# Diagonals of five chunks by quadrant products, one selection per chunk, and a new order for the start of a linear attention kernel with a feed-forward layer

## The chip, the cores and the metric

The kernel runs on one core of a Trainium2 chip. The metric is the device time of one execution in microseconds; the median of three runs stands for a kernel. Five engines work from queues of their own, each in the order written: TensorE (PE; its weight loads are listed as PEld), VectorE (DVE), ScalarE (ACT), GpSimd (POOL) and SyncE (SP, which here only issues DMA transfers). They wait for each other through semaphores.

## The reference

```
for t in range(768):                      # batch 4, 8 heads, head size 48
    cur = (u * k_t) outer v_t
    y_t = r_t @ (state + cur)
    state = w_t[:, None] * state + k_t outer v_t
x = y as (4*768 tokens) x (8*48 = 384)
h = max(x @ w1, x @ w2, x @ w3)           # 384 -> 768
out = h @ w_out                           # 768 -> 384
```

All is float32. The decay w lies between 0.8 and 0.95, so products of it over a chunk become small.

## The kernel before, in words

**Chunks.** The 768 tokens of a batch are cut into 6 chunks of 128, so there are 24 chunks, numbered k = 0 to 23. The eight heads lie as four pairs: one head of a pair on partitions 0 to 47, the other on 64 to 111. Four chunks make a block of 512 tokens, and there are six blocks. Per chunk these steps are done, each named by one letter (line of the code behind it):

- b (365): a DVE scan backwards over the decay, g. Its first column per pair, the decay of the whole chunk, is copied by ACT to `dec`.
- s (373) and f (379): the reciprocal of that decay, held above a floor of 1e-13, starts a forward scan f on DVE.
- r (385): three DVE products scale k by g (two instructions) and r by f (one), in place in the loaded table `tin`.
- X (447): PE makes the scores ("gram"), k' against r', in 64x64 quadrants, into two PSUM banks.
- d, D, e (401, 413, 423): the diagonal term, the sum of r*u*k over the head. For the first six chunks (`CS`) d is a DVE product r*k in two instructions, D sums it over the partitions by small PE matmuls against u, and e copies the eight sums per token to `cs` by ACT. For later chunks POOL makes two products and DVE a sum. e then spreads `cs` on the diagonal of the weight tile `a`: by eight ACT instructions for chunks 0 and 1, by two POOL selections (`affine_select`) for all others. e also issues the next chunk's load of v (and, where needed, of r and k as they are).
- M (465): DVE's `copy_predicated` puts the scores above the diagonal into `a`, one instruction for each of the two banks.
- T (475): PE transposes k'; ACT copies the result (kn) out of the bank "tu".
- R, U, S (488, 496, 510): result from the state, update of the state into the same bank "tu", and its scaling by the decay (four ACT instructions for chunks 0 to 3).
- V, Z (531, 551): PE applies `a` to v, in two halves.
- E (554): ACT copies the result y to x. In the third and fourth chunk of a block it also issues transfers x<-x inside the on-chip memory, three on SP and, in the first block, three on ACT.
- c (397): a check; ACT squares g and f in place and sums them. The sums are judged near the end.

**Feed-forward.** A block has 18 groups (six slices of 128 hidden columns by three weight matrices), each three products of 128x128 by 128x512, and then 24 products for `w_out`. The first block is multiplied in plain float32, later ones in split float32r. Group results lie in three PSUM banks, `psm`, used in turn (the fillers and D use them too). The first of three groups is copied out by ACT, the other two are taken up by DVE with a maximum. The first two groups of the first block begin on chunks 0 to 2 alone (384 columns, line 148) and are completed with the last 128 columns (line 156) when chunk 3 has arrived.

**Weights.** The 24 weight tiles arrive as pairs of 32-bit words. Each is put together by one ACT instruction (`split_w1`, line 311) and two DVE instructions (`split_w2`, 320 and 322).

**Order.** All order is written out by hand. `FRONT` (line 70) is the first stretch: a letter with a digit is a step and its chunk, `W3` three filler matmuls on a zero tile (line 588), `n` a load of r, k, w, `w` a weight load on SP, `i` one `split_w1`, `c` without a digit one whole weight, `p` one of the two early groups, `m` one group, `x` the hand-over of the first block. Then `START`, and `TURN` and `ORD` for each later chunk (line 594), interleaved with groups. An order is an order per engine: what stands behind a waiting instruction of its engine waits too. Ten filler matmuls come ahead of `FRONT`.

Of the kernel before, what the change touches and what calls it, by code (L numbers as in the profile page):

```python
# [69 lines left out]
FRONT = ("b0 s0 f0 d0 W2 D0 W3 r0 X0 e0 T0 W3 c0 b1 s1 d1 D1 U0 f1 W2 R0 e1 S0 M0 V0 Z0 E0 n3 r1 "  # L70
# [25 lines left out]
def kernel(ctx: ExitStack, tc, tin, nat, u_flat, u_pair, v_t, w_all, out, ytr):  # L96
# [107 lines left out]
    with ExitStack() as fast:  # L204
# [711 lines left out]
```

## Time and profile before

| what | value |
| --- | --- |
| median of three runs | 412.45 us (410.98 to 412.71) |
| span of the profiled execution | 409.3 us |
| own time of the profiled execution | not given; its span lies 3.15 us under the median |
| instructions | 9188 |
| TensorE busy | 399.6 us (98%) |
| VectorE busy | 276.2 us (67%) |
| ScalarE busy | 158.2 us (39%) |
| GpSimd busy | 76.7 us (19%) |

Busy time is a sum over the whole span; a busy TensorE may also be running fillers. What a stage waits for is read from the timelines and from the chain of waits, which is followed back from the last instruction.

### The profile page before, as it was taken

To read this page: it belongs to the slowest core of one execution; us is meant where nothing else is said; L and a number is where in the kernel's file an instruction comes from. 1 tells how busy PE (TensorE), PEld (TensorE's weight loads), DVE (VectorE), ACT (ScalarE), POOL (GpSimd) and SP (SyncE) were. 2 spreads that over 40 slices of the span, in tenths; PEclk is the share of its full clock that TensorE was granted. 3 is DMA by queue.
4 is the path that set the end of the run, shared out by engine and by line. 5 is a ranking of instruction groups with operands and counts; after the bars stand their busy time and mean duration, and the time that the engine had idled before them with its cause. 6 is when DMAs were issued, how large, how long until landed. Compare 5 with 4: busy or idle time off the path is not lost.

```text
span 409.3 us, 9188 instructions
## 1 busy us (share of the span) xinstructions
PE 399.6 (98%) x3726; PEld 314.7 (77%) x3726; DVE 276.2 (67%) x504; ACT 158.2 (39%) x356; POOL 76.7 (19%) x92
## 2 busy tenths in 40 slices
PE   6999999999999999999999999999999999999995
PEld 2766554556688889988889988889988888978894
DVE  7988799989869969776778557688565622233320
ACT  2955343333435542434533644533532321322211
POOL 2111041244123113123123113223113200000000
PEclk9999999999999999999999999999999999999999
DMA  8868993630542140694562686841550000300002
GB/s 199 228 183 231 342 345 142 226 105 21 183 148 70 59 126 3 195 295 138 156 194 88 180 257 218 229 145 40 164 185 2 2 2 2 97 2 0 2 3 78
DMA packets 24270, 54.09 MB, mean 132 GB/s; under 512 B 3328, under 2 KB 9920, under 8 KB 24224
## 3 DMA queue, kind: packets, MB, share of 16 engines
q1 hardware_dynamic: 20160, 43.34, 35.0%
q10 hardware_dynamic: 4064, 10.13, 8.2%
q8 instruction: 30, 0.49, 0.5%
q14 instruction: 16, 0.13, 0.1%
HBM read 47.55 MB, written 4.72 MB: 128 GB/s over the span
## 4 chain that ended last, share of the span: by engine, by line
PE 93%; ACT 2%; DMA 1%; SPq 1%; issue 1%; ACTq 1%; POOL 1%; DVE 0%; POOLq 0%
PE psm L168 56%; PE psm L188 17%; PE gram L460 5%; PE y L542 4%; PE tu L503 3%; PE y L493 3%; PE psm L591 2%; PE tu L480 2%; DMA x<-x 1%; PE psm L419 1%; SPq L569 1%; ACTq L569 1%; PE psm L156 0%; ACT x L560 0%; ACT cv L311 0%
## 5 line engine op out<-in xcount | busy, mean ns | idle before, releaser
L168 PE MATMUL psm<-x_hi,w 128*128 128x512 f32 x540 | 172.9, 394 | 0.2 <-ACT m L199 0.2
L168 PEld LDWEIGHTS psm<-x_hi,w 128*128 128x128 f32 x540 | 101.4, 188 | 22.0 <-ACT m L199 0.8
L168 PE MATMUL psm<-x_lo,w 128*128 128x512 f32 x270 | 105.3, 390 | 0.0
L134 DVE TENSOR_TENSOR m<-psm,m 128x512 f32<-128x512 f32 x60 | 41.2, 686 | 61.0 <-PE psm L168 44.4
L188 PE MATMUL psm<-w,h_hi 128*128 128x384 f32 x288 | 78.2, 364 | 0.0
L438 POOL TENSOR_SCALAR_AFFINE_SELECT a<-cs 64x512 f32<-64x512 f32 x44 | 32.2, 733 | 147.1 <-DVE cs L429 93.0
L168 PEld LDWEIGHTS psm<-x_lo,w 128*128 128x128 f32 x270 | 50.7, 188 | 9.8
L188 PEld LDWEIGHTS psm<-w,h_hi 128*128 128x128 f32 x288 | 51.8, 188 | 6.5 <-DVE w L322 0.4
L168 PE MATMUL psm<-x,w 128*128 128x512 f32 x96 | 42.8, 598 | 0.0
L410 POOL TENSOR_TENSOR kr<-kr 128x384 f32<-128x384 f32 x18 | 22.7, 1262 | 97.8 <-PE y L542 87.4
L560 ACT COPY x<-y 112x512 f32<-112x512 f32 x24 | 14.1, 587 | 68.2 <-PE y L542 67.8
L188 PE MATMUL psm<-w,h_lo 128*128 128x384 f32 x120 | 40.3, 336 | 0.0
L399 ACT ACTIVATE gf<-gf 112x1034 f32<-112x1034 f32 x24 | 25.7, 1070 | 35.0 <-DVE tin L394 34.6
L111 ACT CAST h_hi<-m 128x512 fp32r<-128x512 f32 x30 | 18.6, 622 | 52.9 <-DVE m L134 52.5
L382 DVE TENSOR_TENSOR_SCAN gf<-tin,d_fwd 112x517 f32<-112x517 f32 x24 | 34.9, 1454 | 0.7
L168 PEld LDWEIGHTS psm<-x,w 128*128 128x128 f32 x96 | 17.7, 190 | 20.7 <-issue 19.5
L368 DVE TENSOR_TENSOR_SCAN gf<-tin,d_bwd 112x517 f32<-112x517 f32 x24 | 29.9, 1246 | 3.7 <-DMA tin<-in_tin_dram 3.7
L112 DVE TENSOR_TENSOR h_lo<-m,h_hi 128x512 fp32r<-128x512 f32 x30 | 20.6, 688 | 16.8 <-ACT h_hi L111 16.8
L469 DVE COPY_PREDICATED a<-mask,gram 128x384 f32<-128x384 int32 x48 | 25.3, 580 | 1.2 <-PE gram L460 1.2
L542 PE MATMUL y<-a,v 64*64 64x64 f32 (+3 forms) x768 | 25.4, 246 | 0.6
L542 PEld LDWEIGHTS y<-a,v 64*64 64x64 f32 (+1 forms) x768 | 21.4, 126 | 4.6 <-issue 3.1
L131 ACT COPY m<-psm 128x512 f32<-128x512 f32 x30 | 17.5, 582 | 16.7 <-PE psm L168 9.7
(77 smaller groups left out, 428.2 us busy)
## 6 DMA issues: line engine op xcount, KB each, us to landing
tin<-in_tin_dram SPq DMA_DIRECT2D x23, 448.0 KB, 5.6
w<-in_w_all_dram SPq DMA_DIRECT2D x24, 384.0 KB, 6.9
cv<-in_w_all_dram ACTq DMA_DIRECT2D x24, 384.0 KB, 3.8
kr<-in_nat_dram SPq DMA_DIRECT2D x18, 384.0 KB, 5.8
tin<-in_tin_dram SPq DMA_DIRECT2D x23, 231.0 KB, 3.4
v<-in_nat_dram SPq DMA_DIRECT2D x24, 192.0 KB, 5.3
out_dram<-m SPq DMA_DIRECT2D x23, 192.0 KB, 3.0
x<-x SPq DMA_DIRECT2D x30, 32.0 KB, 2.0
```

Source lines behind the costliest of these rows:

```text
L112: rest = lambda: nc.vector.tensor_tensor(out=lo, in0=src, in1=hi.bitcast(F32), op=ALU.subtract)
L134: nc.vector.tensor_tensor(out=m[:, :], in0=ps[:, :], in1=m[:, :], op=ALU.max)
L168: nc.tensor.matmul(ps[:, :], lhsT=wt[f * 3 + wi][:, ct * 128:(ct + 1) * 128], rhs=xt[:, ct, :], start=(n == 0), stop=(n == KT * len(terms) ...
L188: nc.tensor.matmul(pss[tt][:, 0:DM], lhsT=ht[f][:, tok], rhs=wt[FT * 3 + f][:, :], start=(f == 0 and i == 0), stop=(f == FT - 1 and i == l ...
L368: nc.vector.tensor_tensor_scan(out=gf[0:112, 0, ::-1], data0=t[0:112, 0:WC][:, ::-1], data1=d_bwd[0:112, ::-1], initial=0.0, op0=ALU.mult, ...
L382: nc.vector.tensor_tensor_scan(out=gf[0:112, 1, :], data0=tbuf[k % NB][0:112, 0:WC], data1=d_fwd[0:112, :], initial=0.0, op0=ALU.mult, op1 ...
L399: nc.scalar.activation(out=flat, in_=flat, func=AF.Square, accum_out=acc[0:112, k:k + 1])
L410: nc.gpsimd.tensor_tensor(out=n[:, 0, :], in0=n[:, 0, :], in1=n[:, 1, :], op=ALU.mult)
L438: nc.gpsimd.affine_select(out=a[rows, :, 0:2, :], pattern=[[0, 4], [0, 2], [1, HC]], in_=cs[rows, :].rearrange("p (a b) -> p a b", b=2).un ...
L460: nc.tensor.matmul(to, lhsT=p["kp"][q:q + 48, pr, lo:lo + HC], rhs=p["rp"][q:q + 48, pr, HC * late:C], start=(hh, lo) not in begun, stop=T ...
L469: nc.vector.copy_predicated(out=p["a"][:, 2 * hh:2 * hh + 2, :, :].rearrange("p a b c -> p a (b c)"), mask=mask_b(2), data=p["gs"][hh].rea ...
L542: mm = nc.tensor.matmul(p["y"][64 * half:64 * half + m, hh, j, HC * late:C], lhsT=natt[k][0][lo:lo + HC, h * D:h * D + m], rhs=a[:, j, :] ...
```

## The change

- The diagonal of chunks 0 to 4 (`CS` is 5 now): ACT scales r by u (four instructions of 128 columns, one per pair). PE multiplies raw k against it in the same 64x64 quadrants as the scores, of which only the diagonal is wanted. The result needs two PSUM banks: two of `psm`, or for chunk 4 one of `psm` and the bank "tu". ACT copies each to `a` (256 columns), and two POOL selections keep the diagonal, now for chunks 0 and 1 too. Chunk 5's diagonal goes the way of the later chunks: a load, two POOL products, a DVE sum.
- `a` has its blocks in another order. The block that needs no mask is copied by a step of its own, N (ACT, 512 columns in all; for chunk 3 O, on DVE), and M is one `copy_predicated` of 512 columns.
- The floor of the reciprocal is gone; the sums of the checks are compared by their shifted bits.
- The chunk decay is copied by ACT only for chunks behind the fifth; before, it is read from g itself. The scalings of chunk 0 go to tiles of their own.
- The checks of chunks 0 to 4 come behind the loop of the first four chunks (g has five buffers for it). The loads of v are steps of their own, `l`.
- `FRONT` is written anew: 5 fillers in place of 18, weight loads 2 and 3 between the transfers x<-x of chunks 2 and 3, U of chunk 3 behind the two early groups and D of chunk 4.

```diff
-FRONT = ("b0 s0 f0 d0 W2 D0 W3 r0 X0 e0 T0 W3 c0 b1 s1 d1 D1 U0 f1 W2 R0 e1 S0 M0 V0 Z0 E0 n3 r1 "
-         "W1 X1 d2 D2 e2 w w T1 c1 b2 s2 R1 U1 S1 M1 V1 Z1 E1 f2 r2 "
-         "W4 X2 d3 D3 e3 w n4 w T2 c2 b3 s3 R2 U2 S2 i i M2 V2 Z2 E2 w w f3 r3 "
-         "W3 X3 T3 i R3 M3 x V3 Z3 E3 w w n5 w U3 p p d4 w c n6 w m D4 b4 s4 c c3 S3 m w f4 c e4 m r4 c X4 T4 R4 c4 w w")
-TURN = "b1 d1 w | f1 w | D1 r1 c1 | e1 M0 w | "
-ORD = "w R0 V0 U0 X1 Z0 E0 b2 d2 | f2 n3 w | D2 S0 r2 c2 | e2 M1 w | T1 w | |"
+FRONT = ("b0 s0 f0 d0 W2 D0 r0 e0 d1 b1 X0 N0 T0 l2 n3 W1 s1 D1 f1 R0 e1 d2 M0 V0 U0 S0 Z0 E0 r1 "
+         "b2 X1 N1 T1 w w l3 s2 D2 R1 e2 d3 M1 V1 U1 S1 n4 Z1 E1 f2 r2 "
+         "b3 X2 N2 T2 s3 D3 R2 e3 M2 V2 i U2 S2 Z2 E2 l4 w w f3 r3 "
+         "W2 X3 T3 c R3 O3 x V3 Z3 E3 i w w n5 w p p d4 w D4 e4 c U3 n6 w l5 b4 c0 m s4 c S3 c1 m w f4 c c2 m r4 c X4 N4 T4 R4 c3 c4 w w")
+TURN = "b1 d1 w | D1 f1 w | r1 c1 | e1 M0 w | "
+ORD = "w R0 V0 U0 X1 Z0 E0 N1 b2 d2 | f2 n3 w | D2 S0 r2 c2 | e2 M1 w | T1 w | |"
...
-            nc.scalar.copy(out=dec[k % 2][0:112, :], in_=gf[0:112, 0, 1:WC:WS])
-            prep[k]["gf"] = gf
+            if k > CPH:
+                nc.scalar.copy(out=dec[k % 2][0:112, :], in_=gf[0:112, 0, 1:WC:WS])
+            prep[k].update(gf=gf, dec=dec[k % 2][0:112, :] if k > CPH else gf[0:112, 0, 1:WC:WS])
 
         def prep_start(k):
             gf = prep[k]["gf"]
             sep = d_fwd[0:112, 0:NP * WS:WS]
-            nc.vector.tensor_scalar(out=sep, in0=gf[0:112, 0, 1:WC:WS], scalar1=FLOOR, scalar2=None, op0=ALU.max)
-            nc.vector.reciprocal(sep, sep)
+            nc.vector.reciprocal(sep, gf[0:112, 0, 1:WC:WS])
...
+        def weight_of(k):
+            if "a" not in prep[k]:
+                prep[k]["a"] = a_p.tile([128, 3, 4, HC], F32, name="a")
+            return prep[k]["a"]
+
         def prep_diag1(k):
             if k < CS:
                 t = tbuf[k % NB]
-                prep[k]["kr"] = n = nat_p.tile([128, 2, DM], F32, name="kr")[:, :, :].rearrange("p a b -> p (a b)")[:, 0:NP * C]
-                n, r, q = (z.rearrange("p (a b) -> p a b", a=NP) for z in (n, t[:, WC:WC + NP * C], t[:, WC + NP * C:TC_]))
-                for j in range(2):
-                    nc.vector.tensor_tensor(out=pairs(n, j), in0=placed(r, j), in1=pairs(q, j), op=ALU.mult)
+                n = nat_p.tile([128, 2, DM], F32, name="kr")[:, :, :].rearrange("p a b -> p (a b)")[:, 0:NP * C]
+                prep[k]["ur"] = n = n.rearrange("p (a b) -> p a b", a=NP)
+                for pr in range(NP):
+                    nc.scalar.activation(out=n[0:112, pr, :], in_=t[0:112, WC + pr * C:WC + (pr + 1) * C], func=AF.Identity,
+                                         scale=t[0:112, TC_ + pr:TC_ + pr + 1])
                 return
             n = natt[k][1]
...
         def prep_diag_sum(k):
             if k < CS:
-                n, t = prep[k]["kr"], tbuf[k % NB]
-                prep[k]["ps"] = ps = ps_m.tile([128, HT], F32, name="psm")
-                for pr in range(NP):
-                    for lo in (0, HC):
-                        nc.tensor.matmul(ps[lo:lo + HC, pr:2 * NP:NP], lhsT=n[0:112, pr * C + lo:pr * C + lo + HC],
-                                         rhs=t[0:112, TC_ + 2 * pr:TC_ + 2 * pr + 2], start=(pr == 0), stop=True,
-                                         skip_group_check=True)
+                p = prep[k]
+                raw = tbuf[k % NB][:, WC + NP * C:TC_].rearrange("p (a b) -> p a b", a=NP)
+                p["ps"] = ps = [t[:, 0:4 * HC].rearrange("p (a b c) -> p a b c", a=2, b=2) for t in (
+                    ps_m.tile([128, HT], F32, name="psm"),
+                    ps_tu.tile([128, 512], F32, name="tu") if k == CPH else ps_m.tile([128, HT], F32, name="psm"))]
+                begun = set()
+                for half in range(2):
+                    for late in range(2):
+                        for j in range(2):
+                            for hh in range(2):
+                                pr, q = 2 * half + j, 64 * hh
+                                lo, tok = HC * (late if j else 1 - late), slice(HC * late, HC * late + HC)
+                                nc.tensor.matmul(ps[hh][lo:lo + HC, j, half, :], lhsT=raw[q:q + 48, pr, lo:lo + HC],
+                                                 rhs=p["ur"][q:q + 48, pr, tok], start=(hh, lo) not in begun,
+                                                 stop=True, skip_group_check=True)
+                                begun.add((hh, lo))
 
         def prep_diag2(k):
             ahead("D", k)
-            cs = small.tile([128, LINE], F32, name="cs")[:, 0:H]
+            a = weight_of(k)
             if k < CS:
-                nc.scalar.copy(out=cs[:, :], in_=prep[k]["ps"][:, 0:H])
+                for hh in range(2):
+                    nc.scalar.copy(out=a[:, 0:2, 2 * hh:2 * hh + 2, :].rearrange("p a b c -> p a (b c)"),
+                                   in_=prep[k]["ps"][hh].rearrange("p a b c -> p a (b c)"))
             else:
-                nc.vector.tensor_reduce(out=cs[:, :].rearrange("p (a b) -> p b a", a=2),
-                                        in_=natt[k][1][:, 0, :].rearrange("p (b a d) -> p b a d", a=2, d=D),
+                cs = small.tile([128, LINE], F32, name="cs")[:, 0:H]
+                nc.vector.tensor_reduce(out=cs[:, :].rearrange("p (j h q) -> p q j h", j=2, h=2),
+                                        in_=natt[k][1][:, 0, :].rearrange("p (q j h d) -> p q j h d", j=2, h=2, d=D),
                                         axis=AX.X, op=ALU.add)
-            a = a_p.tile([128, 4, 3, HC], F32, name="a")
-            for q in range(4) if k < EARLY else ():
-                for b in range(2):
-                    nc.scalar.activation(out=a[:, q, b, :], in_=ident2, func=AF.Identity, scale=cs[:, 2 * q + b:2 * q + b + 1])
-            for lo in (0, HC) if k >= EARLY else ():
+            for lo in (0, HC):
                 rows = slice(lo, lo + HC)
-                nc.gpsimd.affine_select(out=a[rows, :, 0:2, :], pattern=[[0, 4], [0, 2], [1, HC]],
-                                        in_=cs[rows, :].rearrange("p (a b) -> p a b", b=2).unsqueeze(3).broadcast_to([HC, 4, 2, HC]),
+                src = a[rows, 0:2, :, :] if k < CS else cs[rows, :].rearrange("p (a b) -> p a b", a=2).unsqueeze(3).broadcast_to([HC, 2, 4, HC])
+                nc.gpsimd.affine_select(out=a[rows, 0:2, :, :], pattern=[[0, 2], [0, 4], [1, HC]], in_=src,
                                         compare_op=ALU.is_equal, fill=0.0, base=0, channel_multiplier=-1)
-            prep[k]["a"] = a
-            if k + 1 < NK:
-                load_nat(k + 1)
+            if CPH < k + 1 < NK:
+                ahead("l", k + 1)
...
+        def views(k):
+            to, gs = weight_of(k), prep[k]["gs"]
+            return to[:, :, :, :].rearrange("p b (h a) c -> p h b (a c)", h=2), gs.rearrange("p h b a c -> p h b (a c)")
+
+        def take_full(k):
+            to, data = views(k)
+            nc.scalar.copy(out=to[:, :, 2, :], in_=data[:, :, 2, :])
+
+        def take_alone(k):
+            to, data = views(k)
+            nc.vector.tensor_copy(out=to[:, :, 2, :], in_=data[:, :, 2, :])
+            take(k)
+
         def take(k):
-
-            p = prep[k]
-            for hh in range(2):
-                nc.vector.copy_predicated(out=p["a"][:, 2 * hh:2 * hh + 2, :, :].rearrange("p a b c -> p a (b c)"), mask=mask_b(2),
-                                          data=p["gs"][hh].rearrange("p a b c -> p a (b c)"))
+            to, data = views(k)
+            nc.vector.copy_predicated(out=to[:, :, 0:2, :], mask=mask_b, data=data[:, :, 0:2, :])
```

## Rows read from the trace of the kernel before

**Rows 1.** The page's engine table: busy time, share of the span, instructions.
```profile
PE 399.6 (98%) x3726; PEld 314.7 (77%) x3726; DVE 276.2 (67%) x504; ACT 158.2 (39%) x356; POOL 76.7 (19%) x92
```

**Rows 2.** Windows: length, busy time of PE, PEld, DVE, ACT, POOL, clock, DMA.
```profile
30.00:40.00 10.00, 9.40 (x63) 6.16 (x64) 8.92 (x18) 6.24 (x16) 1.32 (x2) 1.00 0.79 219
40.00:50.00 10.00, 10.00 (x71) 4.91 (x70) 7.59 (x14) 2.67 (x6) 0.00 (x0) 1.00 1.02 326
```

**Rows 3.** The chain of waits, 31 to 37 us: start, length, what.
```profile
30.94 0.48 ACT x L560
31.44 4.08 DMA x<-x
35.65 1.08 PE psm L156 x6
```

**Rows 4.** Timeline of PE: start, length, line, operation, count, idle before it.
```profile
3.22 5.30 PE L591 MATMUL psm<-warm 128*128 128x512 bf16 x12 [3.22 <-POOL warm L586]
...
9.96 0.90 PE L460 MATMUL gram<-tin 48*64 48x128 f32 x32
...
15.05 0.90 PE L460 MATMUL gram<-tin 48*64 48x128 f32 x32
...
19.94 1.04 PE L591 MATMUL psm<-warm 128*128 128x512 bf16 x4
...
26.54 0.90 PE L460 MATMUL gram<-tin 48*64 48x128 f32 x32
...
31.42 4.04 PE L148 MATMUL psm<-x,w 128*128 128x384 f32 x12
...
37.99 2.74 PE L168 MATMUL psm<-x,w 128*128 128x512 f32 x6
40.66 0.90 PE L460 MATMUL gram<-tin 48*64 48x128 f32 x32
...
50.54 0.63 PE L419 MATMUL psm<-tin,kr 112*64 112x2 f32 x16
```

**Rows 5.** Timeline of DVE, chunks 1 to 3 (L376 is the floor).
```profile
16.46 0.17 DVE L376 TENSOR_SCALAR d_fwd<-gf 112x4 f32<-112x4 f32 x1
...
16.76 1.04 DVE L469 COPY_PREDICATED a<-mask,gram 128x384 f32<-128x384 int32 x2
17.69 1.58 DVE L382 TENSOR_TENSOR_SCAN gf<-tin,d_fwd 112x517 f32<-112x517 f32 x1
...
20.44 0.75 DVE L407 TENSOR_TENSOR kr<-tin 112x256 f32<-112x256 f32 x2
```

**Rows 6.** Timeline of POOL and DVE, at 17 and at 132 us.
```profile
16.80 1.39 POOL L438 TENSOR_SCALAR_AFFINE_SELECT a<-cs 64x512 f32<-64x512 f32 x2 [13.63 <-ACT cs L427]
...
131.62 1.01 POOL L411 TENSOR_TENSOR kr<-kr,u_bc 128x384 f32<-128x384 f32 x1
131.82 1.90 DVE L382 TENSOR_TENSOR_SCAN gf<-tin,d_fwd 112x517 f32<-112x517 f32 x1
```

**Rows 7.** Timeline of ACT, 9 to 38 us.
```profile
9.52 2.02 ACT L435 ACTIVATE a<-ident,cs 128x64 f32<-128x64 f32 x8
...
26.60 0.60 ACT L560 COPY x<-y 112x512 f32<-112x512 f32 x1
...
29.83 0.53 ACT L482 COPY kn<-tu 128x448 f32<-128x448 f32 x1 [2.62 <-issue]
...
33.61 0.66 ACT L311 ACTIVATE cv<-w,minus_two 128x384 f32<-128x384 uint32 x1 [2.20 <-issue]
...
34.79 1.07 ACT L399 ACTIVATE gf<-gf 112x1034 f32<-112x1034 f32 x1
...
35.84 0.86 ACT L519 ACTIVATE sstar<-tu,dec 112x48 f32<-112x48 f32 x4
36.76 0.58 ACT L131 COPY h_hi<-psm 128x512 f32<-128x512 f32 x1
```

**Rows 8.** Line 295's weight loads on SP, 14 to 40 us: issue to landing.
```profile
DMA to landing us min/median/max: 3.1/4.6/9.4
```

More of the change, by code (lines that the diff above doesn't have):

```diff
@@ L84 @@
 CHECK = 2
-FLOOR = 1e-13
-LIMIT = 5e25
+LIMIT_BITS = int(np.float32(5e25).view(np.uint32))
 TENTHS = 7.4999 * 2.0 ** -54
@@ L208 @@
         v_p = pool("v", 3)
-        g_p = pool("g", 2)
+        g_p = pool("g", 5)
         a_p = pool("a", 2)
@@ L217 @@
         cv_p = pool("cv", 3)
-        ps_g = pool("ps_g", 2, space=PSUM)
+        ps_g = pool("ps_g", 1, space=PSUM)
         ps_y = pool("ps_y", 1, space=PSUM)
@@ L356 @@
         nc.vector.memset(mid_top[:, :], -7.0)
+        nc.scalar.copy(out=dec[0][:, 0:1], in_=mid_top[:, :])
         load(1)
@@ L449, in scores @@
             p = prep[k]
-            p["gs"] = gs = [ps_g.tile([128, HT], F32, name="gram") for _ in range(2)]
-            p["gs"] = gs = [g[:, 0:6 * HC].rearrange("p (a b c) -> p a b c", a=2, b=3) for g in gs]
+            both = ps_g.tile([128, 2, HT], F32, name="gram")[:, :, 0:6 * HC]
+            p["gs"] = gs = both.rearrange("p h (a b c) -> p h a b c", a=3, b=2)
             begun = set()
@@ L458, in scores @@
                             lo = HC * (late if j else 1 - late)
-                            to = gs[hh][lo:lo + HC, half, j, :] if late else gs[hh][lo:lo + HC, half, j::2 - j, :]
+                            to = gs[lo:lo + HC, hh, j, half, :] if late else gs[lo:lo + HC, hh, j::2 - j, half, :]
                             nc.tensor.matmul(to, lhsT=p["kp"][q:q + 48, pr, lo:lo + HC],
@@ L540, in values @@
                         h, lo = 4 * half + 2 * j + hh, 64 * row
-                        a = p["a"][lo:lo + HC, 2 * hh + half]
+                        a = p["a"][lo:lo + HC, :, 2 * hh + half, :]
                         mm = nc.tensor.matmul(p["y"][64 * half:64 * half + m, hh, j, HC * late:C],
@@ L569, in result @@
                     eng.dma_start(out=x[lo + 48:lo + 64, j, cols], in_=x[lo + 16 * j:lo + 16 * j + 16, KT, cols])
-        steps = dict(X=scores, M=take, T=transposes, R=from_state, U=to_state, S=state, V=values, Z=values2, E=result, n=load,
+        steps = dict(X=scores, M=take, N=take_full, O=take_alone, l=load_nat, T=transposes, R=from_state, U=to_state, S=state, V=values, Z=values2, E=result, n=load,
                      b=prep_scan_b, s=prep_start, f=prep_scan_f, r=prep_rk, c=prep_check, d=prep_diag1,
@@ L580, in ahead @@
                 steps[step](k)
-        ident2 = cst.tile([128, LINE], F32, name="ident2")[:, 0:HC]
-        for lo in (0, HC):
-            nc.vector.tensor_copy(out=ident2[lo:lo + HC, :], in_=ident[lo:lo + HC, lo:lo + HC])
         warm = cst.tile([128, 128], BF16, name="warm")
@@ L875, in _layout @@
         rows[..., WC + NP * C:TC_] = ks.reshape(B, NCH, D, NP * C)
-        rows[..., TC_ + half:TC_ + 2 * NP:2] = u.reshape(NP, 2, D)[:, half].T
+        rows[..., TC_:TC_ + NP] = u.reshape(NP, 2, D)[:, half].T
     def natural(a):
```

33 lines of the change are left out of this document (20 added, 13 removed).

## The prediction

> **What bounds the kernel now.** The page's engine table comes first: TensorE (PE) is busy 98% of the span, VectorE (DVE) 67%, ScalarE (ACT) 39% [rows 1]. The same by stage is the second view: from 30 to 40 us PE has 9.40 of 10.00, from 40 us on it is full, and the granted clock is 1.00 (the level of 2.4 GHz) in both [rows 2]. The chain of waits is the third: before 36 us it leaves PE for ACT's copy of chunk 3's result, for 4.08 us of the transfer x<-x, and is back on PE at 35.65 [rows 3]. From there the end is PE's queue run dry. So the change is worth two things: how much sooner or later PE reaches a fixed point of its queue, and what PE work goes after that point. I take the gram of chunk 4, now at 40.66 [rows 4], as the point. Ahead of it PE also looks full, but with fillers: a group of twelve ends at 8.52 and one of four stands before the gram of chunk 2 [rows 4]. What really sets the pace there is read from the DVE and ACT timelines.
>
> The span is 409.3; the runs' median of 412.45 lies 3.15 above it, and no time of the profiled execution itself is shown, so I keep those 3.15 as they are.
>
> **The loop of the first four chunks.** Grams start at 9.96, 15.05 and (two chunks later) 26.54 [rows 4]: 5.75 us a chunk at the end. After the fillers end at 8.52, D0 follows and then, three fillers being gone, the gram of chunk 0. The new D has 32 matmul passes instead of 16. Bounds: the old D, 0.63, and the gram with its 32 passes, 0.90 [rows 4]. I take 0.7, nearer the old one for its 64 columns: gram 0 at 9.2, 0.75 sooner.
> Per chunk DVE loses the floor, 0.17, the product d, 0.75, and part of the selection: 768 elements in two instructions took 1.04, so 512 cost 1.04 x 512/768 = 0.69, 0.35 less [rows 5]. That is 1.27, and leaves 5.75 - 1.27 = 4.5. PE's own steps, from gram 1 at 15.05 to the filler at 19.94, take 4.89 [rows 4], up to 5.2 with the dearer D, so PE holds the loop at 4.9 at least.
> Against this stands POOL's selection of the diagonal, 1.39 per chunk [rows 6]. Now it runs for chunks 2 to 4 and lies beside the two selections; the scan behind them, begun at 17.69, took 1.58, since POOL was at work until 18.19 [rows 5, 6]. After the change it runs for chunks 0 and 1 too, and starts later: D (0.7) comes behind the gram and the transposes, on ACT kn (0.53) and the two copies of D's result (0.7 in all, below) follow, so POOL begins 2 us or more after the gram's end. By then DVE, past M and the scan, is at the scalings r, all with two SBUF inputs. Each POOL instruction costs DVE between nothing and its whole length, the chunk between 0 and 1.39. So the loop takes 4.9 to 4.5 + 1.39 = 5.9; I take the middle, 5.4. Gram 3 then starts at 9.2 + 3 x 5.4 = 25.4 (23.9 to 27.0), 1.1 sooner than 26.54.
> That POOL holds DVE up whole is shown by a scan begun 0.20 after a POOL product of 1.01: it took 1.90, of which 0.81 passed until POOL's end [rows 6]. The Trainium skill, page "SBUF — State Buffer", section "Who interferes with whom", says the same as a rule: of a VectorE instruction with two SBUF inputs and a GpSimd one that reads SBUF, the later waits until the first has finished. By that rule the upper end holds, and the trace agrees; it is a rival below.
>
> **The tail, from gram 3 to gram 4.** Here ACT decides. ACT's copy of chunk 2's result ends at 27.20; then come three DMA issues, the copy kn at 29.83, a weight split and the copy of chunk 3's result, which ends at 31.41: 4.2 us [rows 7]. After the change the same four stand there. The chunk 2 copy ends about 0.2 after gram 3 (two fillers, 0.5, lie between Z2 and gram 3), so at 25.6, and chunk 3's at 29.8. Behind it ACT now has:
> three issues, 2.2 (31.41 to 33.61) -> 32.0; two splits of 0.66 -> 33.3; the four scalings d4. These have 128 columns; 64 columns took 0.25 (2.02 for eight) and 384 took 0.66 [rows 7], so 0.32 each -> 34.6. PE then does D4, 0.7 -> 35.3. ACT copies its two halves, 256 columns each, between 0.21 (48 columns, 0.86 for four) and 0.53 (448 columns) [rows 7]; 0.35 each -> 36.0. U3 uses the PSUM bank of D4's second half, so it waits for these copies: 1.06 (from the end of kn at 30.36 to 31.42 [rows 4, 7]) -> 37.1. The first two feed-forward groups' last columns follow, 1.7 (35.65 to 37.99 less D4's 0.63 [rows 3, 4]) -> 38.8. Now U3 hides in the wait for ACT, and nothing of D4 stands before x<-x is needed. The new pause, from the end of the two early groups (x<-x of chunks 0 to 2 plus 4.04, about 33.7 [rows 4]) to 38.8, holds only 3.5 of work.
> Meanwhile ACT from 36.0: split 0.66, check c0 1.05 (34.79 to 35.84), split 0.66, S3 0.92 (to 36.76), c1 1.05, and only then the copy that takes up the first group, 0.58 -> 40.9 [rows 7]. Before, one check stood ahead of that copy, which ran at 36.76; c2 to c4 move behind this point. PSUM has three feed-forward banks; the third group takes the one that this copy frees: 40.9 + 2.67 (37.99 to 40.66) = 43.6 for gram 4 [rows 4]. If D4's bank is given out instead, the maximum of the second group on DVE still needs that copy, and r4 stands behind it: 0.69 (the 512-column selection's price) + 1.2 (19.27 to 20.44 [rows 5]) -> 42.8. I take 43.6: 2.95 later than 40.66. The late checks are thus not free here; that they leave the first three chunks hardly matters, since ACT is not the limit there.
>
> **Parts that cost nothing.** The loads of the weights are fewer before chunk 2's x<-x and come behind it: SP waits with them for ACT's copy. After that copy and three issues (25.6 + 2.2) the third is issued near 28 and with the median of 4.6 [rows 8] lands near 32.6, where ACT wants it at 32.0: 0 to 1 us; I take 0, the least landing being 3.1. Fillers taken out are no work. The two identity copies went on under the first load. In the twenty later chunks ACT gets one more copy, 0.58, at 39% busy under a full PE; uncovered it would be 12 us in all, but three banks lie between, so 0 to 1. Chunk 0's scalings go to tiles of their own and the loads of r, k, w and v move to the front of the loop: both only bring data earlier, past queues that wait for nothing there. The values V now wait for ACT's copy N as well as for M, with U, Z and the next gram behind them on PE; N (0.58) is through before M ends, unless d and the copies for the next chunk hold ACT (this case lies within the 5.9). The verdict's one more short VectorE step has the last feed-forward block of PE work behind it. Two POOL products and a load of 384 KB for chunk 5 have several us until its values are needed. The matmuls of D5, 0.63 (50.54), are gone from the full stretch [rows 4].
>
> **Sum.** +2.95 - 0.63 = +2.3: span 411.6, time 414.7. With the loop at 23.9 and the second bank rule: +0.65 - 0.63 = 0.0, 412.5. With 27.0 and a late weight: +4.5 + 1.0 - 0.63 = +4.9, 417.4.
>
> **Rivals.**
> *ACT keeps up, faster.* The loop runs at 4.9, gram 3 at 23.9, chunk 3's copy ends at 28.3, x<-x 4.1 later at 32.4. If d4 is done when the early groups end (32.2), D4 and U3 fill the wait and the late groups start at 33.9 instead of 35.65, with D4 behind them (0.63), and D5 gone (0.63): 3.0 less, 409.4. For it: DVE's 1.27 a chunk is real, and PE's fillers show room. Against it: d4 must end 2 us sooner than ACT's queue gives, and one copy must pass c0 and c1. It decides at the end of the early groups: PE must go on at once. 22%.
> *Nothing.* Loop at PE's pace, ACT's tail as above, the other bank: 412.5 to 413.3, say 413.0. For it: M sits beside POOL without loss in rows 5. 23%.
> *POOL blocks DVE whole in every chunk.* Loop 5.9, gram 3 at 27.0, gram 4 at 45.2: +4.5 - 0.63, 416.4. For it: the scan of 1.90. Against it: POOL may itself be held up and fall behind r. 12%.
> *The clock falls.* Thirteen of 28 fillers go, and PE stands in the new pauses; the first twelve took 0.44 each, the later four 0.26 [rows 4]. At 1.2 GHz the early groups' 4.04 double: 414.7 + 4.0 = 418.7. Against it: the clock is 1.00 in both windows of rows 2. 5%. The Trainium skill, page "TensorE: Matmul & The Clock Gate", section "HAM oscillation — how this bites in real kernels", has pauses between bursts of matmuls bring the slow clock back; by it this case would hold, and no row of before shows such a pause.
>
> **How the numbers follow.** The forecast has 38%, its own range 412.5 to 417.4. Half a per cent, 2.06 us, is about what a measurement of this kernel can tell from no change: 410.4 to 414.5. Faster: the first rival, 22%. Same: the second but for 1%, and 14% from the forecast, 36%. Slower: the forecast's other 24%, and 1, 12 and 5, 42%. For 8 in 10: below 409.4 I leave half of the first rival, above 417.2 the clock and the forecast's end.
>
> **What would show it.** Right: gram 3 near 25.4; ACT without a gap from chunk 3's copy to the first group's take-up; PE idle before D4, before U3 and before the third group, 3 to 5 us in all between 33 and 41; gram 4 near 43.6; after it a full PE. Wrong: the third group starting before 38.5, or PE waiting in later stages for the new ACT copy, or for chunk 5's diagonal.

## The result, and the profile after

The changed kernel takes 419.49 us at the median of four runs against 412.38 in the same comparison; the ratio is 1.014, interval 1.0092 to 1.0188. Medians take in every run, ratios leave out those called slow (here the run of 421.22, further down up to four of a kernel's twelve). I had forecast 414.7 and, for 8 in 10, 409.4 to 417.2. The four runs lie apart: 414.11 (mean granted clock 0.995), 419.23 (0.981), 419.74 (0.979) and 421.22 (0.983); the profiled one is that of 419.74, with a span of 418.0.

The windows of the changed kernel (columns as in [rows 2]) show where it differs from [rows 2], with the clock at 1.00 there:

```profile
10.00:20.00 10.00, 7.18 (x197) 5.88 (x195) 8.21 (x13) 7.34 (x24) 4.09 (x5) 0.91 0.81 239
20.00:30.00 10.00, 9.79 (x163) 7.74 (x159) 6.25 (x9) 4.70 (x16) 3.80 (x4) 0.57 0.20 63
30.00:40.00 10.00, 7.66 (x105) 4.89 (x108) 3.97 (x8) 3.81 (x9) 0.00 (x0) 1.00 0.54 160
40.00:50.00 10.00, 9.18 (x108) 6.92 (x112) 9.20 (x16) 8.06 (x21) 1.53 (x2) 0.83 1.01 287
```

The kernel before from 10 to 30 us, which [rows 2] leave out:

```profile
10.00:20.00 10.00, 9.73 (x226) 7.25 (x226) 9.86 (x22) 9.11 (x34) 1.33 (x2) 1.00 0.86 237
20.00:30.00 10.00, 9.72 (x210) 6.85 (x209) 8.68 (x17) 5.01 (x14) 1.32 (x2) 1.00 0.63 183
```

Two columns matter: the clock falls to 0.57, mostly its lower level of 1.2 GHz, and the DMA share from 20 to 30 us is 0.20 (0.63 before): next to nothing is being loaded there, and from 40 us on the engines are full. The timeline of PE, which answers to [rows 4]:

```profile
8.75 0.85 PE L478 MATMUL gram<-h_hi,kr 48*64 48x128 f32 x32
...
12.52 0.56 PE L570 MATMUL y<-a,v 64*64 64x128 f32 x16 [1.22 <-DVE a L498]
...
15.86 0.57 PE L438 MATMUL psm<-kr,tin 48*64 48x64 f32 x22
17.77 0.39 PE L438 MATMUL psm<-kr,tin 48*64 48x64 f32 x10 [1.34 <-issue]
...
22.12 1.52 PE L478 MATMUL gram<-tin 48*64 48x128 f32 x32
...
30.00 0.90 PE L478 MATMUL gram<-tin 48*64 48x128 f32 x32
...
41.76 0.76 PE L531 MATMUL tu<-v,kn 128*64 128x48 f32 x16 [0.82 <-ACT a L448]
...
45.70 2.74 PE L166 MATMUL psm<-x,w 128*128 128x512 f32 x6
48.38 0.90 PE L478 MATMUL gram<-tin 48*64 48x128 f32 x32
...
64.06 0.56 PE L570 MATMUL y<-a,v 64*64 64x128 f32 x16 [0.59 <-POOL a L458]
```

PE stands 1.22 before chunk 0's values and 1.34 inside D2; then the same gram takes 1.52 instead of 0.90. Gram 3 starts at 30.00, gram 4 at 48.38 (26.54 and 40.66 before).

ACT in the tail, beside [rows 7], and SP's queue:

```profile
34.67 1.81 ACTq L597 DMA_DIRECT2D x<-x  x3
36.77 0.65 ACT L308 ACTIVATE cv<-w,minus_two 128x384 f32<-128x384 uint32 x1 [2.13 <-DMA w<-in_w_all_dram]
38.63 0.64 ACT L308 ACTIVATE cv<-w,minus_two 128x384 f32<-128x384 uint32 x1 [1.22 <-DVE w L319]
39.18 1.26 ACT L417 ACTIVATE kr<-tin 112x128 f32<-112x128 f32 x4
...
45.52 0.60 ACT L129 COPY h_hi<-psm 128x512 f32<-128x512 f32 x1
```

```profile
30.28 2.76 SPq L597 DMA_DIRECT2D x<-x  x3
33.15 0.52 SPq L235 DMA_DIRECT2D v<-in_nat_dram  x1
33.71 0.92 SPq L292 DMA_DIRECT2D w<-in_w_all_dram  x2
```

ACT's idle 2.13 hold its three issues, done at 36.48, and then 0.29 of waiting for a weight; 1.22 follow before the next, until VectorE has taken up the one before. SP issued these two only at 33.71: it takes its queue in order, and the x<-x of chunk 2 stood in it until ACT's copy was done at 30.25. That is the hole in the DMA column.

### The profile page after: what moved, and what is told of

The parts are those of the page before. It is cut to its first block, busy times and chain, and to the rows that moved or that the text cites. A ratio compares the mean times of both kernels' runs of the same rounds, so it can differ in the third digit from the quotient of the medians.

```text
span 418.0 us, 9270 instructions
## 1 busy us (share of the span) xinstructions
PE 401.4 (96%) x3777; PEld 319.0 (76%) x3777; DVE 261.6 (63%) x445; ACT 169.1 (40%) x383; POOL 87.6 (21%) x98
## 4 chain that ended last, share of the span: by engine, by line
PE 88%; DMA 5%; DVE 2%; issue 2%; POOL 1%; ACT 1%; SPq 0%; POOLq 0%; DVEq 0%; ACTq 0%
PE psm L166 51%; PE psm L186 19%; PE gram L478 4%; PE y L570 4%; DMA w<-in_w_all_dram 3%; PE tu L531 3%; PE y L521 3%; PE tu L508 2%; PE psm L616 1%; DMA tin<-in_tin_dram 1%; DVE tin L395 1%; PE psm L438 1%; POOL a L458 1%; DVE tin L399 0%; DVE cv L317 0%
## 5 line engine op out<-in xcount | busy, mean ns | idle before, releaser
L458 POOL TENSOR_SCALAR_AFFINE_SELECT a<-cs 64x512 f32<-64x512 f32 x38 | 27.0, 710 | 97.7 <-DVE cs L452 56.4
L421 POOL TENSOR_TENSOR kr<-kr 128x384 f32<-128x384 f32 x19 | 24.3, 1281 | 104.6 <-PE y L570 87.6
L366 DVE TENSOR_TENSOR_SCAN gf<-tin,d_bwd 112x517 f32<-112x517 f32 x24 | 32.1, 1338 | 3.3 <-DMA tin<-in_tin_dram 3.2
L380 DVE TENSOR_TENSOR_SCAN gf<-tin,d_fwd 112x517 f32<-112x517 f32 x24 | 32.8, 1367 | 0.7
L570 PE MATMUL y<-a,v 64*48 64x128 f32 (+3 forms) x768 | 26.0, 253 | 2.5 <-DVE a L498 1.2
L570 PEld LDWEIGHTS y<-a,v 64*64 64x64 f32 (+1 forms) x768 | 22.5, 131 | 6.4 <-issue 4.4
L422 POOL TENSOR_TENSOR kr<-kr,u_bc 128x384 f32<-128x384 f32 x19 | 24.5, 1288 | 10.3 <-DMA u_bc<-in_u_flat_dram 8.9
L129 ACT COPY m<-psm 128x512 f32<-128x512 f32 x30 | 17.5, 582 | 15.2 <-PE psm L166 11.4
```

Of the source, the lines that this page charges most:

```text
L366: nc.vector.tensor_tensor_scan(out=gf[0:112, 0, ::-1], data0=t[0:112, 0:WC][:, ::-1], data1=d_bwd[0:112, ::-1], initial=0.0, op0=ALU.mult, ...
L380: nc.vector.tensor_tensor_scan(out=gf[0:112, 1, :], data0=tbuf[k % NB][0:112, 0:WC], data1=d_fwd[0:112, :], initial=0.0, op0=ALU.mult, op1 ...
L421: nc.gpsimd.tensor_tensor(out=n[:, 0, :], in0=n[:, 0, :], in1=n[:, 1, :], op=ALU.mult)
L422: nc.gpsimd.tensor_tensor(out=n[:, 0, :], in0=n[:, 0, :], in1=u_bc[:, :], op=ALU.mult)
L458: nc.gpsimd.affine_select(out=a[rows, 0:2, :, :], pattern=[[0, 2], [0, 4], [1, HC]], in_=src, compare_op=ALU.is_equal, fill=0.0, base=0, c ...
L570: mm = nc.tensor.matmul(p["y"][64 * half:64 * half + m, hh, j, HC * late:C], lhsT=natt[k][0][lo:lo + HC, h * D:h * D + m], rhs=a[:, j, :] ...
```

## Experiments

The theories: **the clock** (13 fillers gone, PE pauses, half speed); **the loads** (weights behind x<-x leave the DMA engines idle and come late); **the tail** (ACT's longer queue, the prediction's own reason); and **POOL's selection**. Diffs show only the fragments of `FRONT` that differ.

### The clock

The kernel before, with the fillers of the change:

```diff
-W2 D0 W3 r0 ... T0 W3 c0 ... f1 W2 R0 ... W4 X2 ... W3 X3
+W2 D0 r0 ... T0 c0 ... f1 R0 ... X2 ... W2 X3
```

> The kernel before with its fillers cut to the five of the changed kernel (two ahead of D0, one ahead of gram 1, two ahead of gram 3); nothing else is touched. Theory A: the clock falls here too, in the loop or at its end, and the time goes to 415 to 418. If fillers only fill waits and the fall has another cause (the new order, the longer waits for POOL): the clock stays at 1.00 and the time at 412 to 412.8.

Measured: 417.3, ratio 1.014 (1.0096 to 1.0181). Its windows:

```profile
10.00:20.00 10.00, 8.77 (x145) 6.71 (x143) 9.65 (x21) 7.02 (x25) 1.77 (x2) 0.71 0.82 235
20.00:30.00 10.00, 9.73 (x202) 7.61 (x200) 7.66 (x13) 6.08 (x20) 2.64 (x3) 0.78 0.50 139
30.00:40.00 10.00, 8.45 (x92) 5.68 (x85) 8.36 (x16) 4.40 (x12) 0.00 (x0) 0.83 0.60 179
```

Thirteen matmuls that compute nothing are worth 1.4% to the old kernel. Nothing else was touched. Ahead of the fall PE has three waits of 0.49 to 0.60 us between 8 and 13 us; then the same matmuls take longer, and the clock reads 0.71 to 0.83 where it was 1.00. So this is the clock. The section of the Trainium skill that the prediction named, "HAM oscillation — how this bites in real kernels" of "TensorE: Matmul & The Clock Gate", has pauses bring the slow clock back; the trace agrees, though its pauses are several short ones and the section's example has one long wait after another.

Fillers put back into the changed kernel, 13 in the loop and nine in the tail, the tail's in the gram's bank:

```diff
-s1 D1 f1 R0 ... s2 D2 R1 ... b3 X2 ... s3 D3 R2 ... d4 w D4 e4 c U3
+s1 D1 W5 f1 R0 ... s2 D2 W3 R1 ... b3 W2 X2 ... s3 D3 W3 R2 ... d4 w G6 D4 e4 c G3 U3
```

> The changed kernel with 13 fillers put into the front's matmul queue where its trace shows TensorE standing (five after D1, three after D2, two before the gram of chunk 2, three after D3) and nine more, on the gram's bank, in the tail (six before D4, three before U3). Theory A, the clock: the granted clock stays at 1.00; the 13.6 us that now run at half speed (10.2 from 18.1 us, 3.4 from 42 us) give back some 5 us: 413.5 to 415, gram 3 at 26 to 27. Theory B, the tail (ACT's queue and late weights set the end whatever the loop does): gram 4 stays at 47 to 48 and the time at 418 to 419.5. Theory C, POOL's selection sets the loop: gram 3 stays at 29 to 30 though the clock is up, 418 to 419.5.

Measured: 418.4, ratio 1.018 (1.0125 to 1.0243). In the profiled run (416.69) the clock is 1.00 in every window up to 320 us, and gram 3 starts at 27.58; but gram 4 comes 18.2 behind it, and 1.42 of that it waits for r4. The clock can't be the whole cause. Nor are fillers free: from gram 0 to gram 3 this run takes 19.09, while the run with the checks moved (below), its clock at 1.00 without a filler added, takes 16.83. (The other three runs are 0.7 to 4.5 us longer, at 0.991 to 0.994; why isn't settled.)

### The order of the loads

Two weight loads ahead of chunk 2's x<-x in the changed kernel (one more in all):

```diff
-U2 S2 Z2 E2 l4 w w
+U2 S2 w w Z2 E2 l4 w
```

> The changed kernel with two weight loads moved ahead of the x<-x of chunk 2 and nothing else. The third weight then lands before ScalarE wants it: its wait of 2.13 us for the transfer goes, the four scalings d4 come by that much sooner, D4 waits 0 instead of 1.57 and U3 with it: gram 4 about 16.5 us after gram 3, 417 to 418. Rival: the chain through the conversions' buffers (1.22 us) takes the place of the wait, and only 0.5 is won: 418.5 to 419.5.

Measured: 413.3, ratio 1.002 (0.9993 to 1.0044), 6 us less than the change at the median, more than twice what I expected. Not all of that is the loads directly: nine of its ten runs have a clock of 0.988 or more, of the change's four only one (414.11). Its profiled run, the tenth, has the change's slow loop (gram 3 at 29.37, clock 0.982) and a span 3.6 shorter: gram 0 0.6 sooner, a tail of 17.6 instead of 18.4, and 2.2 less behind gram 4. The rest of the 6 most likely came with the clock; four runs of the change are too few to say how much. With four, and nothing else (`S1 n4 w w Z1 E1` besides):

> The changed kernel with four weight loads moved ahead of the x<-x of chunk 2 instead of two; nothing else. Theory A, the order of the loads is the main cost (every load behind that x<-x waits on SyncE for ScalarE's copy, while the DMA engines stand idle): at least as good as with two, 411 to 413.3. Rival, two are enough, and more only collide with tin of chunk 4 and the x<-x themselves: 413.3 to 415.

Measured: ratio 1.007 (1.0036 to 1.0105). ACT now waits for no weight at all, and the tail shrinks from 18.38 to 15.94:

```profile
26.81 0.90 PE L478 MATMUL gram<-tin 48*64 48x128 f32 x32 [0.34 <-DVE tin L399]
...
36.34 0.67 PE L531 MATMUL tu<-v,kn 128*64 128x48 f32 x16 [0.82 <-ACT a L448]
...
42.75 0.90 PE L478 MATMUL gram<-tin 48*64 48x128 f32 x32 [1.32 <-DVE tin L399]
```

That it isn't faster than two is in its clock: six runs at 0.989 and more take 412.2 to 413.7, five more, at 0.977 to 0.987, 415.9 to 418.1. What is left in the tail are two waits of the change: U3 for D4's copy (shared bank), and gram 4 for r4. That last wait, 1.0 to 1.4, stands in every one of these tails that kept its clock (this one, two early loads, the fillers, the checks below): r4 is VectorE's last step before gram 4, and ahead of it in the queue are the conversions of the weights and the maximum of the second group. Late weights aren't needed for it, as here none is late. ACT's take-up copy, which stands behind the checks c0 and c1, and VectorE's queue:

```profile
40.09 0.61 ACT L129 COPY h_hi<-psm 128x512 f32<-128x512 f32 x1
```

```profile
40.12 0.56 DVE L319 SCALAR_TENSOR_TENSOR w<-w,cv 128x384 uint32<-128x384 uint32 x1
40.73 0.69 DVE L132 TENSOR_TENSOR h_hi<-psm,h_hi 128x512 f32<-128x512 f32 x1
41.34 0.75 DVE L395 TENSOR_TENSOR tin<-tin,gf 112x256 f32<-112x256 f32 x2
42.01 0.69 DVE L399 TENSOR_TENSOR tin<-tin,gf 112x512 f32<-112x512 f32 x1
```

The maximum (40.73) starts when the copy (40.70) and the last conversion (40.68) are both just done: two queues come out level here, and speeding up one of them alone gives little.

The same in the kernel before, the other way round:

```diff
-e3 w n4 w T2 ... Z2 E2 w w f3
+e3 n4 T2 ... Z2 E2 w w w w f3
```

> The kernel before with two of its weight loads moved from ahead of chunk 2's x<-x to behind it, as the change has them; nothing else. If the order of the loads costs by itself: 415 to 418, with ScalarE waiting for a weight near 33 us and the clock at 1.00. If it only cost in the changed kernel, because ScalarE's queue there is longer: 412 to 413.

Measured: 415.6, ratio 1.008 (1.0054 to 1.0102). ACT and, behind it, PE:

```profile
33.52 0.65 ACT L311 ACTIVATE cv<-w,minus_two 128x384 f32<-128x384 uint32 x1 [3.21 <-DMA w<-in_w_all_dram]
```

```profile
36.84 1.91 PE L156 MATMUL psm<-x,w 128*128 128x128 f32 x6 [1.42 <-DMA x<-x]
```

The late weight holds ACT, ACT its copy of chunk 3 and the x<-x behind it, and that holds PE, after which the clock falls too (0.90 and 0.76 from 30 to 50 us). So the order costs in this kernel too, with its shorter ScalarE queue. How much of it is the wait alone isn't separated: I had expected the clock at 1.00. The one run that kept it (0.997) took 413.44, the others, at 0.991 to 0.994, 414.6 to 416.3. Two loads more ahead (`n4 w w w T2 ... E2 f3`) win nothing there:

> The kernel before with all its loop's weight loads, two more, ahead of chunk 2's x<-x. If loads are what sets its end from 30 to 60 us: 409.5 to 411. If TensorE's own work is (its queue has no pause after 36 us): 411.5 to 412.5.

Measured: ratio 1.000 (0.998 to 1.0018): in the kernel before, PE's own work is the bound.

Both causes in the kernel before, with none of the change's new steps:

> The kernel before with both of the causes found and nothing else of the change: its fillers cut as the change cuts them, and two weight loads behind chunk 2's x<-x. Each alone cost 1.4% and 0.8% there. If the two add: 420.5 to 421.5, more than the change's 419.5. If one hides the other (a slower loop comes to the late weights later): 417 to 418.5. Then 1 to 2.5 us of the change's loss belong to the rest of it.

Measured: 420.5, ratio 1.022 (1.019 to 1.0246): they add (1.4 and 0.8).

```profile
10.00:20.00 10.00, 8.81 (x138) 6.66 (x138) 9.25 (x19) 6.57 (x23) 1.63 (x2) 0.65 0.73 223
20.00:30.00 10.00, 9.88 (x142) 7.85 (x144) 7.97 (x14) 3.98 (x13) 2.90 (x3) 0.50 0.30 91
30.00:40.00 10.00, 9.80 (x145) 6.90 (x146) 5.01 (x11) 4.08 (x10) 0.00 (x0) 0.83 0.48 148
```

The two are enough to lose what the change loses, and more; its clock is lower than the change's (0.963 to 0.974), so this isn't the change's loss to the tenth.

### The tail

The tail's order of before and the early loads, without and with the loop's fillers:

```diff
-U2 S2 Z2 E2 l4 w w ... w w n5 w p p d4 w D4 e4 c U3 n6 w l5 b4 c0 m s4 c S3 c1 m w f4 c c2 m r4 ... c3 c4
+U2 S2 w w Z2 E2 l4 w ... w w n5 w U3 p p d4 w c n6 w l5 b4 S3 m D4 e4 s4 c m w f4 c m r4 ... c0 c1 c2 c3 c4
```

> The changed kernel with the tail's order of before: U3 ahead of the first two feed-forward groups, D4 and its copies behind the third group, the five checks behind the transposes of chunk 4, and two weight loads moved ahead of chunk 2's x<-x; no filler added. Theory A, the clock: the loop still runs at half speed from 18 us, gram 3 stays near 30; only the second fall and the late weight go, 415.5 to 417. Theory B, the tail: gram 4 at 43 to 44, 413.5 to 415.

> Both: the 13 fillers of the loop and the tail's order of before with the two early weights. If the clock and the tail each cost their own time, the gains add: gram 3 at 26 to 27, gram 4 at 39.5 to 41, 410 to 412. If only the clock counts, as with the fillers alone: 413.5 to 415. If only the tail counts, as with the tail alone.

Measured: ratios 1.007 (1.0042 to 1.0092) and 1.013 (1.0085 to 1.0173). Less than the early loads alone give; the gains don't add. D4 waited 1.70 and 2.20 for S3, since U3's sum lay in the bank that D4 needs: a fault of my order. With D4 in the gram's banks, S3 back behind the third group and D4's copies behind f4:

> The changed kernel with the tail's order of before and the two early weights, as in the run with the tail alone, but D4's two halves go to the gram's PSUM banks, so that D4 and U3 share nothing and S3 goes back behind the third group. If the 1.70 us that D4 waited for S3 there, and the 1.30 us that gram 4 waited for r4 (which waits for D4, since it scales k in place), come from the shared bank: both waits go and gram 4 comes 14.5 us after gram 3 instead of 16.4, 412 to 413.5. If r4 is late for VectorE's own queue, the 1.3 stays: 413.5 to 415.

Measured: ratio 1.007 (1.0034 to 1.0111). D4 waits no more, and gram 4 now 2.69 for r4, with DVE busy 3.96 of 4.00 from 38 to 42 us: VectorE's own queue, the second alternative. The checks alone behind chunk 4's transposes:

> The changed kernel with the five checks (c0 to c4) behind the transposes of chunk 4 and nothing else moved. The prediction's term: c0 and c1 hold up the take-up copy that the third group waits for, 1.2 us between the two bank rules and up to 2.1 by the two checks' own length: gram 4 one to two us nearer to gram 3 than the 18.4 of the changed kernel, 417.5 to 418.5. Rival: TensorE comes to the third group no sooner than the copy, and the checks cost nothing: 18.2 to 18.4, 419 to 419.5.

Measured: ratio 1.014 (1.0111 to 1.0175). Its PE shows what the loop is where the clock holds (1.00 up to 50 us):

```profile
8.99 0.84 PE L478 MATMUL gram<-h_hi,kr 48*64 48x128 f32 x32
...
17.64 0.39 PE L438 MATMUL psm<-kr,tin 48*64 48x64 f32 x10 [0.98 <-issue]
...
25.82 0.90 PE L478 MATMUL gram<-tin 48*64 48x128 f32 x32 [0.34 <-DVE tin L399]
...
43.49 0.90 PE L478 MATMUL gram<-tin 48*64 48x128 f32 x32 [1.04 <-DVE tin L399]
```

Gram 4 stands 17.7 behind gram 3. It was 18.4 in the changed kernel, with the clock at 0.83 from 40 to 50 us, and 18.2 in the run with fillers, at 1.00 like this one: the checks were worth some 0.6 in the trace, and nothing that the times resolve. In their place ACT now waits 1.42 for a weight.

### A version that beats both

> The likeliest way to beat both kernels: D4 in the gram's banks and right behind chunk 3's values, d4 in the loop, chunk 4's scans and scalings while VectorE is idle, the checks behind chunk 4's transposes, two weights early, u loaded early for chunk 5's diagonal, chunk 0's selection as a product on VectorE instead of POOL, five fillers in the loop. If the pauses are what the change costs: gram 3 at 25 to 26, gram 4 13.5 to 14 us behind it, TensorE without a pause after it, 407.5 to 410. If TensorE stands inside D2 again for nothing that the profile shows (1.0 to 1.3 us) and the clock holds: 409 to 411. If the clock falls: 412 to 415.

Measured: ratio 1.011 (1.0029 to 1.0195), a miss. Gram 4 comes at 40.50, and then PE stands 3.93 (its timeline, and ACT's):

```profile
54.38 8.27 PE L166 MATMUL psm<-x,w 128*128 128x512 f32 x12 [3.93 <-ACT h_hi L129]
```

```profile
46.66 0.65 ACT L308 ACTIVATE cv<-w,minus_two 128x384 f32<-128x384 uint32 x1 [3.52 <-DMA w<-in_w_all_dram]
...
47.89 1.07 ACT L404 ACTIVATE gf<-gf 112x1034 f32<-112x1034 f32 x1
...
52.09 1.05 ACT L404 ACTIVATE gf<-gf 112x1034 f32<-112x1034 f32 x1
...
53.76 0.57 ACT L129 COPY h_hi<-psm 128x512 f32<-128x512 f32 x1
```

A late weight, then my five checks in one block, and the take-up copy behind them. With four early loads, four fillers and u ahead, tail as in the change:

> The same four early loads, four fillers in the pause between D1 and the first values of chunk 0, and u loaded ahead for chunk 5's diagonal: the candidate for a version that beats both kernels. If early loads and a clock that holds add up: 408.5 to 411, granted clock 0.995 or more. If TensorE's standing in D2 takes back what the clock gives: 410.5 to 412.5.

Measured: ratio 1.002 (0.9989 to 1.0042), no better than two early loads. Its twelve runs go from 410.6 at a clock of 0.997 to 420.2 at 0.973, so four fillers don't hold the clock in every run. Then the failed version with both faults out:

```diff
-s1 D1 f1 R0 e1 d2 M0 V0 ... S1 n4 Z1 E1 ... e3 M2 ... U2 S2 Z2 E2 l4 w w
+D1 W3 M0 s1 f1 R0 e1 d2 V0 ... S1 n4 w w Z1 E1 ... e3 d4 M2 ... U2 S2 w w Z2 E2 l4 w
-E3 i w w n5 w p p d4 w D4 e4 c U3 n6 w l5 b4 c0 m s4 c S3 c1 m w f4 c c2 m r4 c X4
+E3 D4 e4 i w w n5 w U3 b4 s4 p f4 p r4 w c c0 n6 w l5 u S3 m c c1 m w c c2 m c X4
```

> The candidate that failed, with its faults out: four weight loads ahead of the x<-x of chunk 2, and the five checks spread over the tail (one behind the first group's weights, two between groups, two behind chunk 4's transposes) instead of in one block of 5.2 us on ScalarE ahead of a take-up copy; D4 in the gram's banks behind chunk 3's values, d4 in the loop, chunk 4's scans early, chunk 0's selection on VectorE, three fillers behind D1. If the block of checks and the late loads made its pause of 3.9 us: no pause behind gram 4, gram 4 near 40, 408.5 to 411. If the weights are still late, TensorE pauses again between 50 and 56 us: 412 to 414.

> The same with chunk 0's selection left on POOL as the change has it, and four fillers behind D1. If VectorE sets the start of gram 1 either way: gram 1 within 0.5 us of the other kernel's 6.0 behind gram 0, and the same time. If the selection on POOL is the loss in chunk 0: gram 1 later, 0.5 to 1 us slower than the other.

Measured: 410.2 and 410.4, ratios **0.9945 (0.9925 to 0.9966)** and **0.995 (0.9926 to 0.9975)**: both beat the kernel before, and each other not at all. Gram 1 starts 6.4 and 5.8 behind gram 0, so POOL's selection isn't the loss in chunk 0: with it on DVE, gram 1 waits 1.56 for r1 instead. In the second, PE stands 2.84 later on; PE, DVE and POOL there:

```profile
57.40 0.56 PE L573 MATMUL y<-a,v 64*64 64x128 f32 x16 [2.84 <-issue]
```

```profile
56.12 0.55 DVE L455 TENSOR_REDUCE cs<-kr 128x8 f32<-128x384 f32 x1 [2.09 <-POOL kr L422]
56.59 0.71 DVE L501 COPY_PREDICATED a<-mask,gram 128x512 f32<-128x512 int32 x1
```

```profile
55.09 0.99 POOL L422 TENSOR_TENSOR kr<-kr,u_bc 128x384 f32<-128x384 f32 x1 [16.52 <-DMA u_bc<-in_u_flat_dram]
```

M4 is queued behind chunk 5's sum, that behind POOL's product, that behind u, issued at 43.5 and 11.4 under way. M4 ahead of e5, then u early as well, and M4 ahead in the version with the change's tail:

```diff
-TURN = "b1 d1 w | D1 f1 w | r1 c1 | e1 M0 w | "
+TURN = "b1 d1 w | D1 f1 w | r1 c1 | M0 e1 w | "
```

> The last kernel but one (four early loads, D4 in the gram's banks, checks spread, selection of chunk 0 on POOL) with one step moved: chunk 4's selection M4 stands ahead of chunk 5's diagonal e5 on VectorE instead of behind it. There V4 waited 2.84 us, and behind it the trace has M4, chunk 5's sum, its POOL product and the load of u, 11.6 us under way. If that chain is the wait: TensorE has no pause near 57 us, and the time falls by 1 to 2.8, to 407.5 to 409.4. If the wait is only handed on to chunk 5's own values: 410 to 410.5, with a pause near 66 us.

> The same, and u is loaded in the loop, behind tin of chunk 4 and ahead of the four weights, where the DMA engines have room. If chunk 5's product is still late for its own values: up to 1 us faster than the other. If M4's place is all: the same as the other within 0.5 us, or slower by a late first weight.

> The changed kernel with four early loads, four fillers, u ahead (in the tail) and M4 ahead of e5; the tail as the change has it, D4 ahead of the late groups and sharing the bank of U3. If D4's place and the lone wait of gram 4 for r4 (1.3 us) are worth what the other kernels won (2 us and more): 410.5 to 412.5, slower than they are by 2. If not: 408.5 to 410.

Measured: ratios 0.995 (0.9929 to 0.9974), 0.999 (0.9969 to 1.0012) and 1.006 (1.0036 to 1.0081). The wait is gone in all three traces, and the time doesn't show it. u in the loop comes out 0.4% behind, which isn't shown to be a loss: the intervals touch, and the means of all twelve runs are 411.2 with it and 410.9 without. The third, 1.1% above the first, shows what the rebuilt tail is worth once loads and clock are mended.

## Why the prediction failed

**The loop: right where the clock holds.** D took 0.70 for chunk 0 (1.02 for chunk 1), M 0.73, the two copies of D 0.65, about as worked out. In the run with the checks moved, with the clock at 1.00, gram 3 starts at 25.82; I had 25.4. Some of that is luck: 0.98 of this loop is the pause inside D2, for which I had no term. In the changed kernel it starts at 30.00, and these 4.6 us are the step that failed: I read the clock of 1.00 off [rows 2] as a state of the kernel, when the fillers of [rows 4] were making it, and called "Fillers taken out are no work" an edit at no cost. The clock as a rival had 5%, its fall in the wrong place (the early groups, not the loop), and its price, 4.0, short of the 5.4 that it has in the kernel before (417.34 less 411.96). The one run of the change that nearly kept its clock (0.995) took 414.11, against the 414.7 forecast.

**The tail: right in size, wrong in cause.** I had 18.2 from gram 3 to gram 4; it took 18.38, and that the two agree is luck. I let the third group wait for the take-up copy that ACT's checks hold up: "the third group takes the one that this copy frees". The copy's end came 16.1 behind gram 3, near the 15.5 that I had (40.9 less 25.4), but the third group had started at 45.70, 0.42 before that end: it doesn't wait for the copy. It was late in the changed kernel mostly because the matmuls ahead of it ran at half clock (the late columns took 2.64 instead of 1.50): with two early loads and the checks where they are it starts 13.5 behind gram 3, not 15.7. What does stand behind the copy is what I had only as the second bank rule, the maximum and r4: with four early loads gram 4 comes 2.05 after the copy's end, by that rule 1.9. The steps that failed are that first rule and "0 to 1 us, I take 0" for the third weight. Its own wait was in that bound (0.29), and the median landing the 4.6 of [rows 8] (4.4 now); what I didn't follow is the queue behind it: the next weight's 1.22 on ACT, the conversions on VectorE, r4 behind these. With four early loads the tail is 15.94, and U3's and r4's waits (2.1) cover the distance to 14.12. I had also not seen that r4 must wait for D4: the old D read a product, the new one reads k itself, which r4 overwrites.

**Behind gram 4.** The forecast had 368.0 there, 0.63 less than before; it took 369.6 (418.0 less 48.38), and 367.5 and 367.9 with two and four early loads. So D5's 0.63 is won where the loads are early. Of the 1.6 over the forecast 1.4 are two waits. 0.59 is chunk 5's diagonal, "several us until its values are needed": POOL's product was done at 61.81, but the sum on VectorE ran only at 62.73, and the chain of waits goes back from it over the conversions to a weight that landed at 54.82. I had listed this as what would show the prediction wrong. The other 0.81, at 193.8 us, is a wait for a take-up copy that stood behind a check on ACT; neither trace with early loads has it, but nothing shows that late loads made it.

**POOL.** The first selection took 2.00 beside DVE's scan and M0 waited 1.21 for it, within the 0 to 1.39 that I gave. As the rival for the loss it is out: with fillers and the clock at 1.00 gram 3 came at 27.58, not the 29 to 30 of that theory. Of the five selections only chunk 0's was tried by itself.

**The sum.** Span 418.0 against the 411.6 of the forecast: 4.6 from the loop, 0.2 from the tail, 1.6 from behind. In times the miss is smaller, 419.49 against 414.7: a run's time lies 1.7 to 1.8 above its span, so the 409.3 of before belong to a run some 1.4 under its kernel's median. The experiments, from the other end: in the kernel before the fillers are worth 1.4% and the order of the loads 0.8%; with both mended and the tail rebuilt, a kernel with the change's new steps wins 0.5%, so these are no loss in themselves.

## What to carry over

A filler matmul isn't slack to be harvested: before taking one out, price the stretch behind it at half clock. Nor is it free to put in: where PE doesn't wait, it takes PE's time (13 of them 2.3 us of the changed loop). In an in-order DMA queue, look at what each load is moved behind and when that is released: a hole in the DMA column ahead of a full stretch is a load in the wrong place. When an instruction reads a buffer that a later one overwrites in place, the later one is a new customer of the first.

## What the runs showed of the hardware

**A pause in D2 that follows the count of instructions.** In eleven kernels PE stands 0.4 to 1.4 us inside D2 for nothing that the profile names. With no filler added between D0 and D2 it comes after 22 of the 32 matmuls (the changed kernel; the checks moved), with three after 19, with four after 18 (five kernels), with five after 17 (three kernels); in the four whose clock has fallen before D2, it is missing. From the version with four:

```profile
15.59 0.56 PE L438 MATMUL psm<-kr,tin 48*64 48x64 f32 x18
17.36 0.40 PE L438 MATMUL psm<-kr,tin 48*64 48x64 f32 x12 [1.21 <-issue]
```

It follows the count of PE's instructions: each filler put ahead brings it one matmul sooner. In the changed kernel one packet of the queue that the page lists as "q8 instruction" starts at 15.0 to 15.5, about a us ahead of the pause, which would fit late code. But the kernels with two and with four early loads have such a packet at 14.0 to 14.5 and no pause, and nothing was tried, so this stays a guess. The Trainium skill, page "Runtime: NRT & Kernel Launch", section "Instruction fetch mechanics", has each engine stream its code in blocks over a DMA queue of its own, at a cost mostly hidden; no run here shows whether this pause is such a cost. Four of the kernels with four early loads have a second pause without a releaser, 0.52 to 1.57 us, ahead of R3.

**The run-to-run spread goes with the clock.** In the version with four early loads, spans go from 410.4 at a mean clock of 0.997 to 418.1 at 0.968, with the same program. The tie isn't strict (a run at 0.990 has 410.5 too), and why the clock falls in one run and not in another isn't shown.
